# Squares in quads, one of eight on ScalarE, one transpose moved to TensorE, and a shifted softmax schedule in a fused attention and channel-mix kernel

## Chip, cores, metric

One NeuronCore of a Trainium2 chip. The metric is the device time of one execution in microseconds (us). The record lists every run used here as fast. So a time is only set against the runs of the kernel before in the same submission, which below is also called "the same chip".

## The reference, cut

```python
# q, k, v: (4, 6208, 256); attention over channels, then a channel mix
qn = q / (norm(q, axis=1) + 1e-06);  kn = k / (norm(k, axis=1) + 1e-06)
s = kn.transpose(0, 2, 1) @ qn / tau            # (B, 256, 256), "covariance"
a = softmax(s, -1)
x = v @ a
x_prev = x shifted by one row
xk = mu_k * x + (1 - mu_k) * x_prev;  xr likewise with mu_r
k = np.maximum(xk @ w_k, 0.0)                   # 256 -> 1024
v = k * k @ w_v                                 # 1024 -> 256
out = sigmoid(xr @ w_r) * v
```

The softmax of a batch needs all rows of its q and k. The kernel therefore runs the channel mix of batch b while it gathers the covariance of batch b + 1.

## The kernel before

The rows are cut into 48 blocks of 512 (12 a batch) and a last block of what is left over. A block takes eight steps (j = 0 to 7 in the code; "step 1" to "step 8" in the prediction). In iteration i the kernel computes `up` of block i + 1 (the relu), `down` of block i (the output) and x of block i + 2; in between come covariance "units" (two matmuls on 128 rows), their sums of squares, and pieces of a softmax.

```python
def up(i, fh):                       # fh = 0..7, one a step
    ...two matmuls of 512 columns into kT_ps...
    nc.scalar.activation(st[i, "kr", fh // 2][:, fh % 2, :m], kT_ps[:, :m], AF.Relu, scale=0.5 ** 0.5)

def square(i, fh):
    m = size(i)
    if fh % 2:                       # a pair: 128x1024
        kr = st.pop((i, "kr", fh // 2))[:, :, :m]
        nc.vector.tensor_tensor(st[i, "kk"][:, fh - 1:fh + 1, :m], kr, kr, op=OP.mult)

def down(i, j):                      # two steps for each 128 rows of the output
    s, h = divmod(j, 2)
    ...if h == 0: two matmuls w_r into vr_ps (two buffers)...
    for fh in (range(3) if h == 0 else range(3, 8)):
        nc.tensor.matmul(vr_ps[:, :D], kk[:, fh, s * P:(s + 1) * P], w_v_sb[:, fh, :],
                         start=fh == 0, stop=fh == 7)

def finish(i, s):                    # frees vr_ps
    nc.scalar.activation(res[:, s], vr_ps[:, D:], AF.Tanh, scale=0.5)
    nc.vector.scalar_tensor_tensor(res[:, s], res[:, s], 1.0, vr_ps[:, :D], op0=OP.add, op1=OP.mult)

# softmax of a batch, one piece a step after its last unit
return [evac, None, fold, None, norms, roots, roots2, None, invert, None, spread, scale,
        None if bounded else top, exp, None, weigh]

# the loop; the order of the calls is the order in each engine's queue
for i in range(-2, NBLK - 1):
    for j in range(8):
        ...finish(i - 1, 3) at j == 1, finish(i, 0..2) at j == 3, 5, 7...
        ...next softmax piece...
        up(i + 1, j)
        ...square(i, 7) at j == 0, else square(i + 1, j - 1)...
        ...down(i, j - 1), at j == 0 down(i - 1, 7)...
        ...x_half(i + 2, 0 or 1) at j == 0, 2; delta at 3; xk at 4, 5; xr at 0, 2...
        ...a covariance unit in some steps; next_add (a 128x1024 fp32 sum on VectorE) at j in (1, 6, 7)...
```

The first multiplies of block i by its squares 4 to 7 come at j = 2, and the last square is queued at j = 0, behind two sums. All VectorE work, `weigh` (which writes the softmax rows `a_sb`) included, runs in the order of the queue. The Trainium skill says so too (TensorE: Matmul & The Clock Gate, "Architectural detail": ScalarE and VectorE are strict FIFO).

Words used below: a *pair*, *triple* or *quad* is one instruction that squares two, three or four of a block's eight 512-column pieces. A *gated output* is the `finish` of 128 rows: a tanh on ScalarE, then a multiply on VectorE, which frees one of the two *output buffers* `vr_ps`. A *sum* is one `next_add`; the *fold* adds the two halves of these sums together for the norms. A name that ends in `_ps` is a tile in PSUM, where this kernel's matmuls write; *evacuating* it is copying it out.

## Time and profile before

Median 516.65 us of three runs (516.42 to 516.98). The profiled execution spans 515.2 us. From its page, the span and the busy time of each engine (in brackets its share of the span):

```profile
span 515.2 us, 9442 instructions
PE 490.6 (95%) x3447; PEld 333.2 (65%) x3509; DVE 457.2 (89%) x788; ACT 431.3 (84%) x858; POOL 104.6 (20%) x143
```

TensorE's 95% is not by itself a measure of distance from the limit; the skill says so (Trainium Kernel Development and Optimization, "Performance Expectations"). I therefore use **late starts**: the time from one matmul's start to the next one's, less 109 ns for 256 columns and 216 ns for 512, summed from the first output multiply of block 0 to the end. These two are the trace's own start distances in undisturbed stretches, and agree with the skill's N/2.4 + 2.5 ns (TensorE: Matmul & The Clock Gate, "Wait — 56ns, not 53.3ns?"), which I take for other widths. An fp32 matmul I count as four; the traces do not show that (such matmuls of 256 columns start 216 ns apart or more), but how they are counted moves all the sums by nearly the same amount (about 0.7 us). (In most traces 58 or 59 of the 784 kT matmuls are missing; where an odd number stands in a run of them, 216 ns are taken off.) Late starts before: 9.89 us of 460.5. That is all that a change of order can win after the loading phase.

The windows view, three whole blocks before, with 6, 4 and no covariance units (columns: us, then busy us and count of PE, weight loads, DVE, ACT, POOL; granted clock; DMA share and GB/s):

```profile
91.17:101.56 10.39, 10.21 (x72) 6.93 (x72) 10.39 (x18) 9.31 (x19) 2.23 (x3) 1.00 1.35 210
201.84:211.40 9.56, 9.51 (x69) 6.65 (x69) 9.35 (x16) 8.45 (x18) 2.24 (x3) 1.00 1.06 173
412.36:421.04 8.68, 8.63 (x61) 5.86 (x60) 7.25 (x13) 7.06 (x16) 0.74 (x1) 1.00 0.76 136
```

The last two rows are pure matmul time: four units are 8 matmuls of 109 ns, and 9.56 - 8.68 = 0.88 us. Six units would take 9.99 us; that block takes 10.39, with VectorE busy in all of it. The waits of TensorE after the first 56 us (total, times, longest):

```profile
PE xT_ps L348 <- DVE a_sb L273: 2.2, 3, 0.9
PE xT_ps L348 <- DMA vT<-v_bf: 1.9, 1, 1.9
PE vr_ps L444 <- DVE res L458: 0.4, 2, 0.2
PE vr_ps L448 <- DVE kk L429: 0.3, 1, 0.3
```

`a_sb` are the softmax rows. The timeline before at the end of the first such softmax:

```profile
156.25 0.69 DVE L429 TENSOR_TENSOR kk<-kr 128x1024 bf16<-128x1024 bf16 x1 [0.16 <-ACT kr L423]
...
156.86 1.22 DVE L154 TENSOR_TENSOR acc<-acc,sq 128x1024 f32<-128x1024 f32 x1
...
157.99 0.41 DVE L458 SCALAR_TENSOR_TENSOR res<-res,vr_ps 128x256 f32<-128x256 f32 x1
...
158.52 0.62 DVE L273 TENSOR_SCALAR a_sb<-s_sb,sm 128x256 bf16<-128x256 f32 x2
...
158.93 0.65 PE L348 MATMUL xT_ps<-vT,a_sb 128*128 128x512 bf16 x2 [0.92 <-DVE a_sb L273]
```

A square, a sum and a gated output stand ahead of the weighing in VectorE's queue, and TensorE idles 0.92 us (1.08 us of late start).

### The profile page before, as it was taken

How to read it: one execution, taken by the hardware profiler on the slowest of the kernel's cores; microseconds unless marked ns; L12 is line 12 of the kernel's file. 1: busy time of each engine (PE TensorE's matmuls, PEld its weight loads, DVE VectorE, ACT ScalarE, POOL GpSimd, SP SyncE). 2: the span in 40 equal slices, each digit the busy share in tenths (PEclk: the TensorE clock that was granted, in tenths of full speed). 3: DMA queues.
4: the chain of work that ended last, by engine and by line, in shares of the span. 5: the costliest groups of instructions: out<-in, count | busy, mean ns of one | idle time of the engine just before them, and what ended most of it. 6: DMA issues, size and time to landing. Idle time of an engine off the chain costs nothing.

```text
span 515.2 us, 9442 instructions
## 1 busy us (share of the span) xinstructions
PE 490.6 (95%) x3447; PEld 333.2 (65%) x3509; DVE 457.2 (89%) x788; ACT 431.3 (84%) x858; POOL 104.6 (20%) x143
## 2 busy tenths in 40 slices
PE   3988899999999999999999999999999999999996
PEld 1453666666666667667666667677666666666665
DVE  3557899999999999999999999999989788888884
ACT  5887889988988889888988898898878887878884
POOL 0045242213242321311243231210030101000000
PEclk9989999999999999999999999999999999999999
DMA  8999999999989999879899999965269676424123
GB/s 298 420 316 181 192 160 192 208 196 193 154 122 188 208 163 190 144 125 193 130 150 188 189 164 169 182 115 130 62 108 178 109 142 117 112 70 116 42 83 102
DMA packets 143734, 83.72 MB, mean 162 GB/s; under 512 B 51716, under 2 KB 140104, under 8 KB 143688
## 3 DMA queue, kind: packets, MB, share of 16 engines
q0 software_dynamic: 65808, 33.01, 51.9%
q1 hardware_dynamic: 77712, 49.98, 41.8%
q8 instruction: 27, 0.44, 0.3%
q14 instruction: 19, 0.16, 0.1%
q10 hardware_dynamic: 168, 0.13, 0.1%
HBM read 78.71 MB, written 25.43 MB: 202 GB/s over the span
## 4 chain that ended last, share of the span: by engine, by line
PE 69%; DVE 16%; DMA 9%; ACT 3%; issue 1%; POOL 0%; SPq 0%; DVEq 0%; ACTq 0%; POOLq 0%
PE vr_ps L448 26%; PE kT_ps L419 23%; PE vr_ps L444 8%; PE xT_ps L348 6%; DMA f<-in_k_dram 5%; PE s_ps L167 5%; DVE acc L154 5%; DVE kk L429 4%; DVE xk L404 2%; DMA v_bf<-in_v_dram 2%; DVE res L458 2%; DMA vT<-v_bf 2%; DVE xr L404 1%; DVE delta L394 1%; ACT kr L423 1%
## 5 line engine op out<-in xcount | busy, mean ns | idle before, releaser
L423 ACT ACTIVATE kr<-kT_ps 128x512 bf16<-128x512 f32 (+1 forms) x392 | 233.9, 600 | 41.0 <-PE kT_ps L419 36.9
L448 PE MATMUL vr_ps<-w_v_sb,kk 128*128 128x256 bf16 x1536 | 231.7, 273 | 0.9 <-DVE kk L429 0.3
L419 PE MATMUL kT_ps<-xk,w_k_sb 128*128 128x512 bf16 (+1 forms) x725 | 218.4, 377 | 0.3 <-DVE xk L404 0.2
L448 PEld LDWEIGHTS <-kk 128*128 128x128 bf16 x1536 | 149.5, 98 | 60.1 <-DVE kk L429 3.0
L429 DVE TENSOR_TENSOR kk<-kr 128x1024 bf16<-128x1024 bf16 (+1 forms) x196 | 133.0, 679 | 4.2 <-ACT kr L423 3.3
L458 DVE SCALAR_TENSOR_TENSOR res<-res,vr_ps 128x256 f32<-128x256 f32 x192 | 79.7, 415 | 28.2 <-ACT res L457 27.8
L419 PEld LDWEIGHTS <-w_k_sb 128*128 128x128 bf16 x784 | 76.1, 98 | 28.6 <-issue 0.5
L154 DVE TENSOR_TENSOR acc<-acc,sq 128x1024 f32<-128x1024 f32 x69 | 84.0, 1217 | 0.0
L167 PE MATMUL s_ps<-qk 128*128 128x256 bf16 (+1 forms) x392 | 74.0, 291 | 5.4 <-DVE qk L131 5.4
L457 ACT ACTIVATE res<-vr_ps 128x256 f32<-128x256 f32 x192 | 75.4, 393 | 1.3 <-PE vr_ps L448 1.3
L444 PE MATMUL vr_ps<-w_r_sb,xr 128*128 128x256 bf16 x384 | 73.2, 272 | 3.1 <-DVE res L458 0.4
L350 ACT CAST xT<-xT_ps 128x512 bf16<-128x512 f32 x94 | 55.8, 594 | 23.3 <-PE xT_ps L348 23.1
L150 ACT ACTIVATE sq<-qk 128x1024 f32<-128x1024 bf16 (+1 forms) x72 | 75.2, 1046 | 0.0
L404 DVE SCALAR_TENSOR_TENSOR xr<-delta,mu_t,xT 128x512 bf16<-128x512 bf16 x96 | 71.4, 744 | 0.0
L404 DVE SCALAR_TENSOR_TENSOR xk<-delta,mu_t,xT 128x512 bf16<-128x512 bf16 x96 | 71.3, 745 | 0.0
L444 PEld LDWEIGHTS <-xr 128*128 128x128 bf16 x384 | 37.5, 98 | 45.4 <-issue 1.4
L125 POOL DMA_DIRECT2D qk<-in_q_dram x39 | 28.7, 736 | 181.1 <-ACT kr L423 140.5
L348 PE MATMUL xT_ps<-vT,a_sb 128*128 128x512 bf16 x188 | 56.1, 379 | 4.1 <-DVE a_sb L273 2.2
L311 POOL DMA_DIRECT2D v_bf<-in_v_dram x48 | 37.2, 777 | 67.8 <-DMA vT<-v_bf 62.6
L167 PEld LDWEIGHTS <-qk 128*128 128x128 bf16 (+1 forms) x392 | 39.0, 103 | 17.9 <-DVE qk L131 8.2
L394 DVE TENSOR_TENSOR delta<-xT 128x1024 bf16<-128x1024 bf16 x48 | 32.9, 686 | 0.1
L133 ACT ACTIVATE qk<-f 128x1024 bf16<-128x1024 f32 (+2 forms) x28 | 25.9, 947 | 7.4 <-DMA f<-in_q_dram 4.1
(82 smaller groups left out, 164.1 us busy)
## 6 DMA issues: line engine op xcount, KB each, us to landing
out_dram<-res SPq DMA_DIRECT2D x47, 512.0 KB, 5.2
v_bf<-in_v_dram POOLq DMA_DIRECT2D x48, 256.0 KB, 7.7
qk<-in_q_dram POOLq DMA_DIRECT2D x36, 256.0 KB, 6.3
qk<-in_k_dram POOLq DMA_DIRECT2D x36, 256.0 KB, 7.4
f<-in_q_dram SPq DMA_DIRECT2D x11, 512.0 KB, 8.4
f<-in_k_dram SPq DMA_DIRECT2D x11, 512.0 KB, 9.3
vT<-v_bf SPq DMA_TRANSPOSE x45, 7.9
f<-in_q_dram SPq DMA_DIRECT2D x2, 256.0 KB, 8.3
```

The source lines that it names most:

```text
L150: nc.scalar.activation(t[:rows], qk[:rows, s:s + min(n, 2)].rearrange("p s i c -> p s (i c)"), AF.Square)
L154: nc.vector.tensor_tensor(sums[b], sums[b], t, op=OP.add)
L167: nc.tensor.matmul(s_ps[:, ih, :], qk[:rows, s, 1, ih * P:(ih + 1) * P], qk[:rows, s, 0, :], start=t0 and ih == 0, stop=te, skip_group_che ...
L348: nc.tensor.matmul(xT_ps, a_sb[:, b, ih, dh * P:(dh + 1) * P], vT[:, :, ih, :], start=ih == 0, stop=ih == 1)
L404: nc.vector.scalar_tensor_tensor(o[:, dh], st[i, "d"][:, dh], mu[:, dh:dh + 1], st[i, "x"][:, dh, :M], op0=OP.mult, op1=OP.add)
L419: nc.tensor.matmul(kT_ps[:, :m], w_k_sb[:, dh, fh * P:(fh + 1) * P], xk[:, dh, :m], start=dh == 0, stop=dh == 1)
L423: nc.scalar.activation(st[i, "kr", fh // 2][:, fh % 2, :m], kT_ps[:, :m], AF.Relu, scale=0.5 ** 0.5)
L429: nc.vector.tensor_tensor(st[i, "kk"][:, fh - 1:fh + 1, :m], kr, kr, op=OP.mult)
L444: nc.tensor.matmul(vr_ps[:, D:], xr[:, dh, s * P:(s + 1) * P], w_r_sb[:, dh, :], start=dh == 0, stop=dh == 1)
L448: nc.tensor.matmul(vr_ps[:, :D], kk[:, fh, s * P:(s + 1) * P], w_v_sb[:, fh, :], start=fh == 0, stop=fh == 7)
L457: nc.scalar.activation(res[:, s], vr_ps[:, D:], AF.Tanh, scale=0.5)
L458: nc.vector.scalar_tensor_tensor(res[:, s], res[:, s], 1.0, vr_ps[:, :D], op0=OP.add, op1=OP.mult)
```

## The change

Intent: take load off VectorE where it bounds (fewer, longer squares, one in eight on ScalarE while covariance runs), have the softmax rows sooner, and drop the wait for one DMA transpose. The cut leaves out the new steps of the units from block 8 on, and the change of `FOLD` and `holds` that goes with them; the comments are added.

```diff
-        return [evac, None, fold, None, norms, roots, roots2, None, invert, None, spread, scale,
-                None if bounded else top, exp, None, weigh]
+        return [evac, fold, None, None, norms, roots, roots2, None, None, invert, None, None, spread,
+                scale, *([] if bounded else [top]), exp, None, weigh]
...
-        if fh % 2 == 0:
-            st[i, "kr", fh // 2] = p2.tile([P, 2, M], BF16, name="kr", tag="kr", bufs=3)
+        if fh % 4 == 0:
+            st[i, "kr", fh // 4] = p2.tile([P, 4, M], BF16, name="kr", tag="kr", bufs=2)
...
+        if fh == 0 and by_act(i):                  # by_act: 1 <= i < 3 * NB - 2
+            nc.scalar.activation(st[i, "kk"][:, 0, :m], kr, AF.Square)
...                                                # square(): n = 4
+            lo = 1 if fh == 3 and by_act(i) else fh % 4 + 1 - n
+            kr = st[i, "kr", fh // 4][:, lo:fh % 4 + 1, :m]
+            nc.vector.tensor_tensor(st[i, "kk"][:, fh // 4 * 4 + lo:fh + 1, :m], kr, kr, op=OP.mult)
...
-            if i == -1 and j == 6:
-                v_transpose_pe(2, nc.vector.tensor_copy)()
+            if (i, j) in ((-1, 6), (0, 4)):
+                v_transpose_pe(i + 3, nc.vector.tensor_copy)()
...
-                slots = (3, 5, 7)                  # units: i == 0, 1, < 8, then by place in the batch
-                slots = (1, 2, 4, 5, 7)
+                slots = (3, 5, 6, 7)               # batch 1 now ends at i = 7, j = 4, not j = 7
+            elif i < 7:
                 slots = (1, 2, 3, 4, 5, 7)
...
-            if adds and adds[0][0] <= now[0] and (j in (1, 6, 7) or adds[0][1] == holds[0] and chain):
+            if adds and adds[0][0] <= now[0] and (j in (1, 6, 7) or j == 2 and adds[0][1] == holds[0] and chain):
```

More of the change, by code (lines that the diff above doesn't have):

```diff
@@ L420, in up, with by_act @@
                              start=dh == 0, stop=dh == 1)
-        if fh % 2 == 0:
-            st[i, "kr", fh // 2] = p2.tile([P, 2, M], BF16, name="kr", tag="kr", bufs=3)
-        nc.scalar.activation(st[i, "kr", fh // 2][:, fh % 2, :m], kT_ps[:, :m], AF.Relu, scale=0.5 ** 0.5)
+        if fh % 4 == 0:
+            st[i, "kr", fh // 4] = p2.tile([P, 4, M], BF16, name="kr", tag="kr", bufs=2)
+        kr = st[i, "kr", fh // 4][:, fh % 4, :m]
+        nc.scalar.activation(kr, kT_ps[:, :m], AF.Relu, scale=0.5 ** 0.5)
+        if fh == 0 and by_act(i):
+            nc.scalar.activation(st[i, "kk"][:, 0, :m], kr, AF.Square)
+    def by_act(i):
+        return 1 <= i < 3 * NB - 2
     def square(i, fh):
         m = size(i)
-        if fh % 2:
-            kr = st.pop((i, "kr", fh // 2))[:, :, :m]
-            nc.vector.tensor_tensor(st[i, "kk"][:, fh - 1:fh + 1, :m], kr, kr, op=OP.mult)
+        n = 4 if i < NBLK - 1 else 2
+        if fh % n == n - 1:
+            lo = 1 if fh == 3 and by_act(i) else fh % 4 + 1 - n
+            kr = st[i, "kr", fh // 4][:, lo:fh % 4 + 1, :m]
+            nc.vector.tensor_tensor(st[i, "kk"][:, fh // 4 * 4 + lo:fh + 1, :m], kr, kr, op=OP.mult)
     def down(i, j):
@@ L542 @@
     chain = []
-    FOLD = 14
-    holds = [0]
+    FOLD = 16 if bounded else 17
+    holds = [0, 0]
     def unit(ahead=2):
@@ L557, in unit @@
             chain.extend(softmax_pieces(u[0]))
-            holds[0] = u[0]
+            holds[:] = u[0], now[0] + 4
     def next_load():
@@ L633 @@
                 mix(i + 1, "xr", int(j > 0))
-            if i == -1 and j == 6:
-                v_transpose_pe(2, nc.vector.tensor_copy)()
-            if j == 5 and 3 <= i + 4 < NBLK - 1:
+            if (i, j) in ((-1, 6), (0, 4)):
+                v_transpose_pe(i + 3, nc.vector.tensor_copy)()
+            if j == 5 and 4 <= i + 4 < NBLK - 1:
                 v_transpose(i + 4)
@@ L645 @@
             elif i == 0:
-                slots = (3, 5, 7)
-            elif i == 1:
-                slots = (1, 2, 4, 5, 7)
-            elif i < 8:
+                slots = (3, 5, 6, 7)
+            elif i < 7:
                 slots = (1, 2, 3, 4, 5, 7)
-            else:
-                slots = (3, 5, 7) if (i - 8) % NB == 0 else (1, 3, 4, 5, 7) if (i - 8) % NB < 3 else (1, 3, 5, 7)
-            if j in slots and pos["mm"] < len(units):
+            elif i == 7:
+                slots = (1, 2, 3, 4)
+            elif (i - 7) % NB == 0:
+                slots = (5, 7)
+            else:
+                slots = (1, 3, 4, 5, 7) if (i - 7) % NB in (1, 3, 6, 9) else (1, 3, 5, 7)
+            if j in slots and pos["mm"] < len(units) and now[0] >= holds[1]:
                 unit()
-            if adds and adds[0][0] <= now[0] and (j in (1, 6, 7) or adds[0][1] == holds[0] and chain):
+            if adds and adds[0][0] <= now[0] and (j in (1, 6, 7) or j == 2 and adds[0][1] == holds[0] and chain):
                 next_add()
```

## The prediction

> What bounds it now. The page: TensorE busy 95%, VectorE 89%, ScalarE 84%. In the timeline 256-column matmuls start every 109 ns and 512-column ones every 216 ns, the back-to-back rate that the Trainium skill gives (TensorE: Matmul & The Clock Gate, "Wait — 56ns, not 53.3ns?"). Take a block as the time between the first output multiplies of successive blocks on VectorE: without covariance it takes 8.68 us, with four units 9.56, just its matmul columns at that rate. From 57.8 us on, what starts later than that rate sums to only 9.9 us:
> - 2.1 us at 63.1 us: the fourth block's v landed at 55.9, its DMA transpose took 9.4 us (chain of waits).
> - 2.9 us in 70 to 143 us, batch 1's covariance. Six units should take 9.99 us; blocks take 10.39, VectorE 100% busy (windows), ScalarE idle 1.08. TensorE waits 0.2 us a block for the last squared pair.
> - 2.7 us at 158, 275 and 390 us: a batch's first x matmul waits for the softmax rows (1.08 + 1.08 + 0.54).
> - The rest: small waits. The first 55 us hardly change.
>
> What changes.
> 1. Squares. VectorE starts its next instruction 0.60 us after a pair (timeline) and 512 elements take 418 ns, 1024 take 684 (groups by shape), 0.52 ns an element: a quad about 1.22 us long (1.13 apart), a triple 0.95 (0.87). Four pairs cost 2.40 us a block, triple plus quad 2.00, two quads 2.27. The saving is the fixed part (the skill's VectorE: DVE Perf Modes, "The TRN2 errata"). ScalarE gets 33 squares of 128x512; a 64x512 one took 620 ns, about 0.5 us apart. A six-unit block's VectorE falls from 10.39 to 9.99, ScalarE rises from 9.31 to 9.8, TensorE needs 9.99: three engines level, so I expect 10.05 to 10.2. Counter-effect: half of a block's squares now waits for one quad; in four-unit blocks the last pair ended 0.64 us before its use; the quad should just fit.
> 2. v of block 3: the 2.1 us wait goes; eight transposes cost TensorE about 0.45 us. Blocks 0 and 1 then hold ten units, not eight, plus the new squares: about 22 us of ScalarE work for 20 us of matmuls, so about 1 us comes back as waits for evacuated PSUM.
> 3. Schedule. Batch 1's last unit moves from step 8 to step 5 of its block, but the fold waits two steps for sums: the rows are still weighed in the same step, with one square less before them; batches 2 and 3 weigh one step (1.2 us) sooner. I expect 0.7 of 1.08 back for batch 1, nearly all for the others.
>
> Sum: transposes and early blocks -0.8; batch 1 blocks -1.5 (with that stage's end); softmax rows -2.3; small waits -0.3. About -4.9 us.
>
> Predicted 511.8 us, 80% range 509.5 to 514.0. Faster by over 2% (below 506.3) 3%. Within 2% 96%. Slower 1%.
>
> What would show it. Right: no TensorE wait for the DMA transpose; waits for softmax rows under 0.6 us in total; six-unit blocks near 10.1; squares about 1.22 and 0.95 us; ScalarE without idle time from 60 to 80 us; four-unit blocks still 9.56, plain ones 8.68. Wrong: four-unit blocks at 9.6 or more (quad), or six-unit ones at 10.3 (ScalarE).
>
> What would make it wrong. A late ScalarE in batch 1 delays the tanh and thereby VectorE and the quads. Should ScalarE's allowed lag hide the early overload: 510.

## The result

The changed kernel took 515.06 us (median of four, 514.76 to 516.78), the kernel before 516.59 us (four runs). The ratio is 0.9976, interval 0.9954 to 0.9999. A ratio is the mean time of one kernel's runs over that of the other's of the same rounds, so it is not quite the ratio of the medians quoted. The gain is 1.2 us by the ratio and 1.5 us by the medians where 4.9 were predicted, and 515.06 lies above the predicted range. The profiled execution is the slowest of the four (516.78 us); it holds a spell of half clock that is taken up under after_again.

The page after:

```profile
span 515.0 us, 9327 instructions
PE 490.3 (95%) x3456; PEld 333.5 (65%) x3517; DVE 442.2 (86%) x693; ACT 446.8 (87%) x891; POOL 103.3 (20%) x143
```

VectorE lost 15 us of busy time, ScalarE gained 15.5, and the span hardly moved. The windows of blocks with 6, 4 and no units:

```profile
91.87:101.86 9.99, 9.94 (x73) 6.99 (x72) 9.99 (x16) 9.64 (x21) 2.72 (x4) 1.00 1.47 184
202.30:211.86 9.56, 9.45 (x67) 6.55 (x68) 8.94 (x13) 8.90 (x19) 2.23 (x3) 1.00 0.95 148
412.05:420.73 8.68, 8.63 (x61) 5.88 (x60) 7.04 (x11) 7.06 (x16) 0.74 (x1) 1.00 0.70 139
```

The six-unit block is now at its 9.99 us of matmuls. Groups by shape after (count, busy us, mean ns):

```profile
L437 DVE TENSOR_TENSOR kk<-kr 128x2048 bf16<-128x2048 bf16 x63 | 76.8, 1220 | 2.3 <-ACT kr L424 2.3
L437 DVE TENSOR_TENSOR kk<-kr 128x1536 bf16<-128x1536 bf16 x33 | 31.4, 951 | 0.0
L426 ACT ACTIVATE kk<-kr 128x512 bf16<-128x512 bf16 x33 | 20.8, 630 | 1.1
```

The instruction costs came as predicted. But the waits of TensorE after 56 us are new ones:

```profile
PE vr_ps L456 <- DVE kk L437: 1.4, 3, 0.6
PE vr_ps L456 <- DVE xT L341: 0.8, 1, 0.8
PE xT_ps L348 <- DVE a_sb L273: 0.5, 1, 0.5
PE vr_ps L452 <- DVE res L466: 0.4, 1, 0.4
PE kT_ps L419 <- ACT kr L424: 0.4, 1, 0.4
```

The second line names a memset of `xT`, which the multiplies do not read. It is the profile's guess from times: the memset (278.27 us) ran in the last moments of the square that really ended the wait. The timeline after, at the end of the second softmax, shows what it was:

```profile
273.95 0.62 DVE L273 TENSOR_SCALAR a_sb<-s_sb,sm 128x256 bf16<-128x256 f32 x2
...
274.49 1.22 DVE L154 TENSOR_TENSOR acc<-acc,sq 128x1024 f32<-128x1024 f32 x1
...
274.65 1.11 ACT L424 ACTIVATE kr<-kT_ps 128x512 bf16<-128x512 f32 x2
...
275.11 0.59 PE L348 MATMUL xT_ps<-vT,a_sb 128*128 128x512 bf16 x2
...
275.95 1.22 DVE L154 TENSOR_TENSOR acc<-acc,sq 128x1024 f32<-128x1024 f32 x1
...
277.09 1.22 DVE L437 TENSOR_TENSOR kk<-kr 128x2048 bf16<-128x2048 bf16 x1
277.29 0.27 PE L456 MATMUL vr_ps<-w_v_sb,kk 128*128 128x256 bf16 x1
...
278.37 0.50 PE L456 MATMUL vr_ps<-w_v_sb,kk 128*128 128x256 bf16 x3 [0.81 <-DVE xT L341]
```

The rows are in time (the x matmul at 275.11 does not wait). But VectorE then does two sums before the quad, and the multiply by square 4 waits until the quad has ended at 278.31. ScalarE had delivered the last relu by 275.76, so it was not the cause here. The same holds for every wait for a quad over 0.2 us in this profile (six, at 69, 79, 140, 150, 161 and 278 us): VectorE went to the quad straight from another instruction, and the relu before it had ended 0.53 to 1.66 us earlier.

Late starts by stage (us, from the traces; "no_schedule" and "weigh_next" are experiments below):

| stage (blocks of the output) | before | after | after, 3rd profile | no_schedule | weigh_next |
|---|---|---|---|---|---|
| 0-1, early | 2.09 | 1.13 | 1.19 | 0.85 | 0.63 |
| 2-7, covariance of batch 1 | 2.00 | 0.50 | 0.50 | 0.51 | 0.08 |
| 8-12, softmax 1 | 2.68 | 2.87 | 2.87 | 1.74 | 1.15 |
| 20-24, softmax 2 | 1.90 | 1.68 | 1.67 | 1.68 | 0.98 |
| 32-36, softmax 3 | 1.21 | 1.14 | 1.14 | 1.15 | 0.58 |
| all others | 0.03 | 0.23 | 0.22 | 0.65 | 0.38 |
| sum | 9.89 | 7.56 | 7.60 | 6.59 | 3.80 |

About 1.5 to 1.7 us in each column are the softmax's own small and fp32 matmuls. The last four columns have eight transposes more (0.45 us of work).

### The profile page after: what moved, and what is told of

Read it like the earlier page. It is cut to its first block, busy times and chain, and to the rows that moved or that the text cites. A ratio compares the mean times of both kernels' runs of the same rounds, so it can differ in the third digit from the quotient of the medians.

```text
span 515.0 us, 9327 instructions
## 1 busy us (share of the span) xinstructions
PE 490.3 (95%) x3456; PEld 333.5 (65%) x3517; DVE 442.2 (86%) x693; ACT 446.8 (87%) x891; POOL 103.3 (20%) x143
## 5 line engine op out<-in xcount | busy, mean ns | idle before, releaser
L437 DVE TENSOR_TENSOR kk<-kr 128x1536 bf16<-128x1536 bf16 (+2 forms) x100 | 109.9, 1099 | 2.3 <-ACT kr L424 2.3
L350 ACT CAST xT<-xT_ps 128x512 bf16<-128x512 f32 x94 | 55.3, 589 | 14.7 <-PE xT_ps L348 14.5
```

The lines of the kernel that those rows point to most:

```text
L437: nc.vector.tensor_tensor(st[i, "kk"][:, fh // 4 * 4 + lo:fh + 1, :m], kr, kr, op=OP.mult)
```

## Experiments

Theory A: VectorE's backlog decides. The second half of a block's squares is now one quad at the end of VectorE's queue, and whatever is moved ahead of it comes back as a wait for it. Theory B, the rival: ScalarE's new squares make relu and tanh late. Theory C: the wait for the DMA transpose hid other lags. Fifteen runs were made, all correct, each with five rounds (two of them, after_again and after_third, are the changed kernel once more); "late" is the sum of late starts.

| run | median us (before) | ratio to before, 95% | late us |
|---|---|---|---|
| q_only | 517.05 (515.31) | 1.0031 (1.0005-1.0057) | 10.48 |
| q_and_a | 513.33 (515.31) | 0.9961 (0.9939-0.9982) | 6.64 |
| t_only | 515.64 (515.31) | 0.9998 (0.9976-1.0020) | 8.19 |
| s_only | 515.31 (515.31) | 0.9993 (0.9970-1.0016) | 8.64 |
| after_again | 513.79 (515.69) | 0.9963 (0.9950-0.9976) | 7.19 |
| no_schedule | 513.09 (515.69) | 0.9954 (0.9941-0.9966) | 6.59 |
| late_sums | 513.45 (515.69) | 0.9956 (0.9944-0.9968) | 6.88 |
| last_in_pairs | 514.76 (515.69) | 0.9983 (0.9969-0.9997) | 7.46 |
| rows_sooner | 514.51 (514.84) | 0.9993 (0.9978-1.0007) | 8.19 |
| ladder2 | 512.69 (514.84) | 0.9961 (0.9944-0.9978) | 5.46 |
| ladder3 | 512.09 (514.84) | 0.9945 (0.9932-0.9958) | 5.39 |
| ladder4 | 511.28 (514.84) | 0.9932 (0.9916-0.9948) | 4.01 |
| exp_in_place | 512.57 (517.06) | 0.9917 (0.9897-0.9937) | 4.04 |
| weigh_next | 511.49 (517.06) | 0.9896 (0.9880-0.9912) | 3.80 |
| after_third | 515.45 (517.06) | 0.9967 (0.9954-0.9980) | 7.60 |

### The parts one by one

**q_only**: the changed kernel with these undone: ScalarE's square, the transpose, the schedule.

```diff
-        return 1 <= i < 3 * NB - 2
+        return False          # and the old slots, pieces, sums and DMA transpose
```

> Before, with the squares in two quads a block on VectorE, nothing on ScalarE, old schedule, old transposes. Theory A (the last quad is late, behind VectorE's long sums, and half of the next multiplies wait for it): six-unit blocks at about 10.26 us instead of 10.39, but the multiplies by the last quad wait more than by the last pair after each softmax, so 0 to -0.6 us against before. Theory B (the squares on ScalarE delay everything): none of it here, so the whole 0.13 us a block in the covariance stage of batch 1 shows, about -0.8 us, and no wait for a quad in the block after a softmax is longer than the 0.2 us of the pair.

Measured: slower than before by 0.3% (late 10.48). Six-unit blocks took 10.25 us as expected, but TensorE waited for the quad in all of them (0.13 to 0.50 us) and after the first two softmaxes (0.31 and 0.48 us each time). So both theories missed the sum. A had the place right. B's sign, that no wait for a quad there is longer than 0.2 us, is refuted: the quad is late without any square on ScalarE. Late starts are 0.6 us over those of before, by the clock it is 1.6 us; these waits do not explain the rest.

**q_and_a**: the same with ScalarE's square (`by_act` as in the change).

> Before, with the squares as in the change (triple and quad on VectorE, one of eight on ScalarE), old schedule, old transposes. Theory A: six-unit blocks at 9.99 to 10.05, -2 us there, and 0.5 to 1 us given back in waits for the last quad: -1 to -1.5 us. Theory B: ScalarE's new squares delay the relus that the quad needs, so it is no better than the quads alone, and TensorE waits for the evacuation of PSUM by ScalarE by more than 1 us in total.

Measured: -2.0 us by the ratio, late 6.64; six-unit blocks 9.99. Waits for PSUM evacuation by ScalarE sum to 0.02 us. B is refuted: with the square on ScalarE the squares pay, without it they do not. Against q_only late starts fell by 3.84 us; 1.69 of that is a DMA wait which q_only happened to have (below), and 2.2 us is the square's. A's prediction holds, a little better than expected.

**t_only**: before, with only the transpose of v of block 3 on TensorE.

```diff
+            if (i, j) in ((-1, 6), (0, 4)):
+                v_transpose_pe(i + 3, nc.vector.tensor_copy)()
```

> Before, with v of block 3 transposed on TensorE only. If the wait of 2.1 us for the DMA transpose is simply gone and eight transposes cost 0.45 us: -1.6 us. Theory C (that wait hid lag of ScalarE and VectorE in the first blocks, which now shows as other waits): -0.2 to -0.8 us, with new TensorE waits for squares or PSUM between 60 and 80 us that sum to over 0.8 us.

Measured: no gain by the clock (0.9998), though its trace has no wait for v and only 0.17 us of late starts in blocks 0 and 1. Neither expectation fits. The reason shows in the other traces of the same chip, which still use the DMA transpose. The times (us) at which v of block 3 and its transpose landed, and what TensorE waited:

| run | v landed | transpose landed | late start at the first x matmul of block 3 |
|---|---|---|---|
| before (first profile) | 55.9 | 65.3 | 2.09 |
| q_only | 55.8 | 64.7 | 1.69 |
| q_and_a | 54.3 | 63.6 | 0 |
| s_only | 54.2 | 63.3 | 0 |

The wait that I counted as a fixed 2.1 us is a race between a DMA landing and TensorE, decided anew in each run. In half of these four profiles there was nothing to win, and the transposes then cost their 0.45 us. Theory C's new waits of over 0.8 us are not there either; its "-0.2 to -0.8 us" lies within the interval of the ratio (-1.2 to +1.0 us), so by the clock it stays open.

**s_only**: before, with only the schedule of the change (units, sums, pieces).

> Before, with the schedule of units, sums and softmax pieces of the change only (pairs as before). Theory A: with pairs the softmax rows come in time and nothing new is waited for: waits for the rows of batches 2 and 3 fall from 1.6 to under 0.3 us, total -1.2 to -1.8 us. Rival (the new order of sums and softmax work itself is what makes the squares late, quads or not): waits for the pair after the softmax of 0.5 us or more appear here too, total 0 to -0.6 us.

Measured: 0.9993, no gain. The waits for the rows of batches 2 and 3 are gone, as A said. In their place TensorE starts late for an output buffer (0.58 us near 276, 0.35 near 137) and for the pair at the end of batch 1 (0.74 us near 140, in the block where the fold now stands before it). The rival in the expectation was right about the total: the new order makes its own waits, quads or not. Its sign was not quite met: the long wait after the softmax is for an output buffer, behind a pair and a sum in VectorE's queue (the tanh had ended 1.3 us before the output began), and that for a pair there is 0.22 us.

### The whole change again, and without one part

**after_again**: the changed kernel, unchanged.

> The changed kernel once more, to stand beside the next ones on the same chip. Its first profile had a spell of half TensorE clock at 52 to 55 us, in the midst of dense matmuls, where the others have theirs before 39 us. If that was chance: no such spell after 40 us here, 1 to 1.5 us less up to the first output multiply, and -1.5 to -2.5 us against before. If the change causes it, it is there again.

Measured: -1.9 us, first output multiply at 53.8 us instead of 56.3. The spell was not there again, nor in the third profile, so the change does not bring it about by itself. In the first profile TensorE had waited 1.84 us for v of block 2 and then ran at half clock for 3.4 us, as the timeline of the first profile shows:

```profile
51.80 0.97 PE L327 MATMUL vT_ps<-ident,v_bf 128*128 128x128 bf16 x8 [1.84 <-DMA v_bf<-in_v_dram]
52.57 1.49 PE L167 MATMUL s_ps<-qk 128*128 128x256 bf16 x6
53.85 1.76 PE L419 MATMUL kT_ps<-xk,w_k_sb 128*128 128x512 bf16 x4
```

Four 512-column matmuls take 1.03 us elsewhere. The late starts after it are the same in the three profiles of this kernel within 0.4 us, and the two long waits (0.97 and 0.80 us) return to 0.01 us.

**no_schedule**: the change without its schedule.

> The change without its schedule of units, sums and softmax pieces: squares and the transpose of v of block 3 only. Theory A (the schedule gives nothing, since VectorE is behind in the softmax blocks whatever the order, and its fold and two sums ahead of the quad at the end of batch 1 cost 1 us): 0.5 to 1.2 us faster than the changed kernel, late starts in blocks 8 to 12 about 1.8 us instead of 2.9. Theory B (schedule useful, its worth hidden by ScalarE's new squares): slower than the changed kernel by 0.5 us or more.

Measured: 0.7 us under the changed kernel by the medians (the intervals overlap), late 6.59 against 7.19; blocks 8 to 12: 1.74 us instead of 2.87. By late starts the change's schedule costs time: the three softmax stages lose 4.57 us without it and 5.69 with it. By the clock this is likely but not shown. The 0.8 us wait near 139 us (fold and two sums ahead of the quad) is not there.

**late_sums**: the changed kernel with the sums kept out of the end of two softmax blocks.

```diff
-            if adds and adds[0][0] <= now[0] and (...):
+            if adds and adds[0][0] <= now[0] and not (i in (NB - 3, 2 * NB - 3) and j > 4) and (...):
```

> The changed kernel, but in the two blocks that end a softmax (covariance still running) no sum of squares is added in their last three steps; the two sums come in the next block. Theory A (VectorE's backlog, 2.3 us of sums ahead of the quad, makes the wait): the TensorE wait for the quad near 278 us goes from 0.97 to under 0.2 us, that near 161 us from 0.31 to 0, that for the rows near 159 us from 0.62 to under 0.2; -1 to -1.6 us against the changed kernel, unless the sums then make the next quads late. Theory B (ScalarE late with the relu): the waits stay within 0.3 us of what they were.

Measured: the waits near 278 and 161 us vanish, as A predicted and B did not. But two of 0.18 and 0.42 us appear in the next blocks, where the sums are made up, and the wait for the rows of batch 1 stays 0.62 us; the whole is 0.3 us, not 1 to 1.6. The timeline of this run at that wait showed a second cause:

```profile
152.60 0.19 ACT L266 ACTIVATION_READ_ACCUMULATOR s_sb<-s_sb,rn 128x1 f32 x1
...
154.59 0.38 ACT L465 ACTIVATE res<-vr_ps 128x256 f32<-128x256 f32 x1
...
155.01 0.42 DVE L466 SCALAR_TENSOR_TENSOR res<-res,vr_ps 128x256 f32<-128x256 f32 x1 [1.07 <-ACT res L465]
...
155.35 0.16 DVE L271 RECIPROCAL sm<-sm 128x2 f32<-128x2 f32 x1
155.54 0.86 DVE L273 TENSOR_SCALAR a_sb<-s_sb,sm 128x256 bf16<-128x256 f32 x2
```

The exponentials were done at 152.8, VectorE was idle from 153.9, and the weighing still waited: it stood in the queue behind an output whose tanh ended at 155.0. With the sums away, TensorE's wait comes of the queue's order, not of VectorE's load (weigh_next below tests this).

**last_in_pairs**: the changed kernel with squares 4 to 7 in two pairs.

```diff
-        n = 4 if i < NBLK - 1 else 2
+        n = 4 if i < NBLK - 1 and fh < 4 else 2
```

> The changed kernel with the second half of the squares as two pairs again (triple, pair, pair in the covariance stages). Theory A: the wait near 278 us goes from 0.97 to about 0.3 us and the ones at the end of batch 1 and in the first blocks shrink by half, but six-unit blocks take 10.12 us again (VectorE +0.13): together -1 to 0 us against the changed kernel. Theory B (ScalarE): the waits stay, and with VectorE's extra 0.13 us a block it is slower by 0.5 us or more.

Measured: about 1 us slower than the changed kernel by the medians, 0.3 us by late starts. The wait near 278 us became two of 0.71 (for the output buffer) and 0.22 us (for the pair), and the wait for batch 1's rows doubled to 1.36 us, a pair more standing ahead of the weighing. A's total was wrong and B's (slower by 0.5 us or more) came true, but not for B's reason: the buffer at 273.85 us waited for an output that stood behind a pair and a sum on VectorE, 1.4 us after its tanh had ended. So the length of the quad alone is not the trouble; what fits is the amount of VectorE work between two deadlines.

### Toward a version that works

**rows_sooner**: no_schedule, with exp and weigh one step sooner.

```diff
-                None if bounded else top, exp, None, weigh]
+                *([] if bounded else [top]), exp, None, weigh]
```

> The change without its schedule (the run no_schedule), but exp and the weighing of the rows one step sooner (exp from step 6 to 5 of its block, weighing from step 8 to 7), so that the weighing stands ahead of a gated output in VectorE's queue, not behind it. In the run late_sums VectorE idled 1.07 us for that output's tanh while the exponentials of batch 1 were long done. Theory A2 (place in the queue, behind the tanh or a sum): the waits for the rows of batches 1 and 2, 0.50 us each in no_schedule, go; the two sums now both stand between the rows and the quad, so waits for the quad of 0.3 us rise to 0.8; net -0.6 to +0.3 us against no_schedule (6.6 us of late starts there). Rival (exponentials late on ScalarE): the waits for the rows stay at 0.5 us.

Measured: a miss. No wait for rows is left, but late starts rose from 6.59 to 8.19 us and the gain over before was lost (0.9993). The quad's waits rose to 0.97 us, and new ones came up for the output buffer, 0.46 and 0.25 us in each of two softmaxes. The timeline of this run:

```profile
149.16 0.49 ACT L266 ACTIVATE s_sb<-s_sb,rn 128x256 f32<-128x256 f32 x1
...
150.13 1.05 ACT L150 ACTIVATE sq<-qk 128x1024 f32<-128x1024 bf16 x1
...
151.08 0.37 ACT L465 ACTIVATE res<-vr_ps 128x256 f32<-128x256 f32 x1
...
151.48 0.42 DVE L466 SCALAR_TENSOR_TENSOR res<-res,vr_ps 128x256 f32<-128x256 f32 x1 [0.72 <-ACT res L465]
...
151.95 0.38 PE L452 MATMUL vr_ps<-w_r_sb,xr 128*128 128x256 bf16 x2 [0.30 <-DVE res L466]
```

In its new step exp stands ahead of a tanh on ScalarE; VectorE idles 0.72 us for that tanh, and TensorE waits for the buffer that the output frees.

**ladder2**: rows_sooner, with the second x matmul before the multiplies by the quad.

```diff
+            if j == 2 and 0 < i + 2 < NBLK - 1:
+                x_half(i + 2, 1)
             if j > 0 and i >= 0:
                 down(i, j - 1)
...                                                # the old call after it is taken out
```

> rows_sooner, and in step 3 of each block TensorE does the second x matmul (0.43 us) before the multiplies by the last quad, not after. Nothing is added. Theory A (the last quad ends too late by 0.1 to 1 us, once or twice a batch and in the first blocks): each wait for a quad shrinks by 0.43 us, those of 0.1 to 0.5 us vanish; late starts for squares fall by 1.2 to 2 us in total, and the time with them. Theory B (ScalarE bounds there): the waits turn up at the next matmul, total unchanged within 0.4 us.

Measured: late 5.46 instead of 8.19 us, time -1.8 us against rows_sooner on the same chip. The first blocks' and the covariance stage's waits for the quad are gone (0.5 us down to 0.08 in blocks 2 to 7). A holds, more than expected: the quad was late by a few tenths, and 0.43 us of other TensorE work covers that. B is refuted once more.

**ladder3**: ladder2, with `by_act` up to `3 * NB + 1`.

> ladder2, and ScalarE does its square in three more blocks, past the end of covariance (the last softmax). The wait of 0.57 us near 386 us there (TensorE waits for a gated output behind a quad in VectorE's queue) should fall by the 0.27 us by which a triple is shorter; nothing else changes: -0.2 to -0.3 us against ladder2, within noise by the clock, so it is judged by the late starts.

Measured: late starts 0.07 us less. The wait it aimed at had already gone from 0.57 to 0.08 us with ladder2, a side effect that I had not foreseen. The medians differ by 0.6 us, but the intervals overlap, so this edit's worth stays unproved.

**ladder4**: ladder3, with the sums put off as in late_sums.

> ladder3, and the two sums at the end of the two softmax blocks put off into the next block, as in late_sums. Theory A: what is left of waits for the quad after the softmax (0 to 0.5 us each) goes, and the later quads, which the sums delay, have the 0.43 us from the reordering to spare: -0.3 to -0.9 us against ladder3. Total for this kernel: late starts 3.3 to 4.3 us (1.5 of them the small matmuls of the softmax), 510 to 511.5 us where before takes 515.7.

Measured: late 4.01 us, 511.28 us where before takes 514.84; no wait for a quad over 0.1 us is left. Late starts are as expected; the gain of 3.6 us over before is less than the 4.2 to 5.7 that the expected times implied.

**exp_in_place** and **weigh_next**: exp_in_place is ladder4 with the pieces of before; weigh_next moves only the weighing:

```diff
-                None if bounded else top, exp, None, weigh]
+                None if bounded else top, exp, weigh]
```

> ladder4 with the softmax pieces back at their old steps (exp in step 6 after the tanh, weighing in step 8 behind a gated output): separates what moving the rows sooner cost. Theory (exp in an even step stands ahead of a tanh on ScalarE, VectorE then idles 0.7 us for that tanh, and TensorE waits 0.35 to 0.7 us a batch for a free output buffer): the two waits of 0.35 us near 152 and 269 us go; but the rows come behind the tanh again, so a wait of 0.3 to 0.6 us for the rows of batches 1 and 2 returns. Net within 0.5 us of ladder4's 4.0 us of late starts.

Measured: the waits of 0.35 us are gone, which ties them to the place of exp. The rows' wait came back at only 0.11 us, less than expected (late 4.04 us).

> exp_in_place, but the rows weighed in the step right after exp (step 7), ahead of the gated output in VectorE's queue; exp stays after the tanh. Same theory: neither the waits for the output buffer (0.35 us twice) nor those for the rows (over 0.2 us) are left, late starts 3.0 to 3.5 us, about 510.5 us where before takes 515. Rival (exp takes too long, so that VectorE idles for it at the weighing): the wait for the rows stays at 0.3 us or more, or later outputs are delayed as much.

Measured: late 3.80 us, a little over the range, since 0.34 us of waiting for ScalarE remained in the first blocks. There is no wait for the rows and none for the buffer at exp; 0.25 and 0.11 us for the buffer remain two blocks later, where the sums are made up, as in ladder4. The ratio is 0.9896, so it takes 5.4 us less than before. The timeline at the end of the first softmax, and all that the waits view lists after 56 us:

```profile
151.30 0.50 ACT L266 ACTIVATE s_sb<-s_sb,rn 128x256 f32<-128x256 f32 x1
...
152.54 0.62 DVE L273 TENSOR_SCALAR a_sb<-s_sb,sm 128x256 bf16<-128x256 f32 x2
...
152.75 0.40 ACT L465 ACTIVATE res<-vr_ps 128x256 f32<-128x256 f32 x1
...
153.18 0.42 DVE L466 SCALAR_TENSOR_TENSOR res<-res,vr_ps 128x256 f32<-128x256 f32 x1
...
154.01 0.59 PE L348 MATMUL xT_ps<-vT,a_sb 128*128 128x512 bf16 x2
```

```profile
PE vr_ps L452 <- DVE res L466: 0.3, 2, 0.2
PE kT_ps L419 <- ACT kr L424: 0.2, 1, 0.2
```

The weighing now falls into time in which VectorE would have waited for the tanh.

**after_third**: the changed kernel on the same chip as these two.

> The changed kernel as it is, to compare the best version with it on one chip: 1.5 to 2 us under before, 2 to 3.5 us over the two above.

Measured: 1.7 us under before by the ratio; exp_in_place is 2.9 and weigh_next 4.0 us under it by the medians, the latter a little more than expected.

## Why the prediction was wrong

The step that failed is the third one, the schedule: "softmax rows -2.3". The waits for the rows did fall by 2.1 us (late starts 2.70 to 0.62), but nearly as much came back at the next deadlines in VectorE's queue. Nearly every sign that the prediction had named for being right was there (no wait for the transpose, the rows at about 0.6 us, blocks of 9.99, 9.56 and 8.68 us, squares of 1.22 and 0.95 us, ScalarE without idle time from 60 to 80 us), and the time was still wrong: each sign looked at one wait, none at what the moved work would delay.

By the late starts of the first two profiles, the predicted sum and the measured one stand so:

| term | predicted us | measured us |
|---|---|---|
| transposes and early blocks | -0.8 | -0.5 (2.09 to 1.13, plus 0.45 of transposes) |
| batch 1 blocks | -1.5 | -1.5 (2.00 to 0.50) |
| softmax rows, and small waits beside them | -2.6 | -0.1 (5.79 to 5.69 in three stages) |
| other stages | 0 | +0.2 |
| sum | -4.9 | -1.9 (by the clock -1.5, in later pairs -1.9 and -1.7) |

- **What bounds, and costs of instructions: right.** TensorE's matmul rate bounds: plain blocks stayed at 8.68 and four-unit ones at 9.56 us (two of them at 9.66). The quad took 1.22 us and the triple 0.95, exactly as worked out. Pairs, triples and quads all fit 0.52 ns an element and some 0.15 us fixed, which agrees with the Trainium skill (VectorE: DVE Perf Modes, "The TRN2 errata": a measured fixed term of about 150 cycles at 0.96 GHz, estimated 156 ns). ScalarE's 512-element square took 630 ns; the skill's 186 ns + 0.833 ns an element for scale and bias given as immediates (ScalarE: Activation LUTs, "What ACT_TABLE_LOAD costs") gives an estimate of 613.
- **Batch 1's blocks: right in size**, and a little better in kind: 9.99 us, no loss from three level engines.
- **Softmax rows: the step that failed.** "I expect 0.7 of 1.08 back for batch 1, nearly all for the others." The rows did come in time for batches 2 and 3 (their wait went from 1.08 and 0.54 us to none), but little was won, since 0.97 us of waiting for the quad (batch 2) and 0.56 for an output buffer (batch 3) took its place. Batch 1 got back 0.46 us (1.08 to 0.62) of the 0.7 expected, against new waits for quads of 0.26 and 0.31 us. Much of this is the schedule's own doing: without it (no_schedule) the three stages lose 4.57 us, with it 5.69, before 5.79; the other stages lose 0.4 us more without it. I looked at each deadline of TensorE alone. VectorE does its work in one queue, with several deadlines close together (rows, quad, output buffers), and moving one piece ahead moves the others back. rows_sooner and late_sums show it from both sides.
- **"The quad should just fit": failed.** I had checked it in four-unit blocks, where it does fit within 0.1 us (near 210 and 327 us TensorE waits that long for it). In the blocks after a softmax, at the end of batch 1 and in the first blocks it was late by 0.3 to 1.0 us.
- **The schedule at the end of batch 1: failed, and I had seen its cause.** I noted that the fold waits for sums, but not that fold and sums then stand straight ahead of a quad: 0.81 us where the pair of before was 0.44 us late; gone without the schedule (no_schedule).
- **v of block 3: mechanism right, size not general.** The wait was 2.1 us in the profile that I read, 1.7 in another and none in two. An average over runs was needed, and one profile cannot give it. The 1 us that I expected back from ScalarE's overload was 1.13 us of late starts in blocks 0 and 1 (0.78 in a second profile), of which 0.59 is the quad's, behind a sum on VectorE, and 0.54 a wait for PSUM that ScalarE evacuates.

Left open: how much the DMA transpose's race is worth on average, and whether ladder3's edit does anything. The half-clock spell of the first profile was not repeated, no run was made to provoke it, and its cause stays open.

## What to carry to other kernels

Where a strict-order engine feeds a bound one, list all its deadlines around the place you change, and count the work between them: a piece moved ahead of one deadline is a delay of the next. Look for order as well as load: putting a ready piece ahead of an instruction that waits for another engine, and doing other matmuls before the ones that wait, won some 3 us here (no_schedule to weigh_next, by their ratios, the sums put off and ladder3's edit included). The whole change had won 1.2 to 1.9 us. The load mattered too: the squares with ScalarE's share alone won 2.0 us (q_and_a). A wait on a DMA landing that one profile shows should be looked up in several before a saving is booked on it.

## What the Trainium skill lacked or had wrong

- TensorE: Matmul & The Clock Gate, "Back-to-back issue gap", gives about 131 ns for sustained 512-column matmuls in a stream with weight loads. Here such a stream, with a weight load for each matmul, starts one every 216 ns (and 109 ns for 256 columns); a block of 8.68 us is just that rate. The page's own "isolated" formula is the one that holds in the stream.
- The same page, "What's actually happening", has the clock go to half after at least one idle window of about 3.4 us. In the first profile after the change the matmuls' idle time before the spell (51.9 to 55.3 us by the trace's clock record) was 1.84 us, and the spell lasted 3.413 us. That is all the idle time in the 3.4 us before the spell. What counts as idle the trace does not show.
- No page has that a profile's releaser may be a bystander: a 0.81 us wait was put down to a memset of 0.06 us that began 0.04 us before the end of the square that really ended it.
- VectorE: DVE Perf Modes has the fixed cost that longer instructions save, but does not set against it that what reads the first part of a long result waits for its end: here the multiply by square 4 waited 0.97 us for the quad's end at 278.31 us. Two quads instead of four pairs saved VectorE 0.13 us a block, and that kernel was 0.3% slower (q_only; interval 0.05 to 0.57%).
